# An mLSTM cell and a Fourier-mixed MLP on one core: MLP input products in pairs, the feature transform at half the frequencies, one PSUM pool of four banks

## The chip, the cores and the metric

The kernel runs on one core of a Trainium2 chip. Its engines work side by side, each with a queue of its own that it goes through in order: TensorE (PE in the profile, its weight loads PEld), VectorE (DVE), ScalarE (ACT), GpSimd (POOL) and SyncE (SP), which issues the DMAs here. The metric is the device time of one execution in microseconds, median of the runs. All data is fp32, and each fp32 product shows up in the trace as two weight loads and two matmuls ("passes").

## The reference

An mLSTM cell over 4 batches, 8 heads, 768 steps and 40 features a head gives x of 4 x 768 x 320; then a Fourier mix and an MLP:

```python
for t in range(S):
    m_new = np.maximum(f_gate[:, :, t] + m, i_gate[:, :, t])
    f_stab = np.exp(f_gate[:, :, t] + m - m_new)
    i_stab = np.exp(i_gate[:, :, t] - m_new)
    C = f_stab[:, :, None, None] * C + i_stab[:, :, None, None] * np.einsum('bhd,bhe->bhde', vt, kt)
    n = f_stab[:, :, None] * n + i_stab[:, :, None] * kt
    ...
    y[:, :, t] = o * h_tilde / denom
x = y.transpose(0, 2, 1, 3).reshape(B, S, H * D)
X = np.fft.fft(x, axis=1)
X = np.fft.fft(X, axis=2)
u = x + np.real(X)
mu = np.mean(u, axis=-1, keepdims=True)
var = np.mean((u - mu) ** 2, axis=-1, keepdims=True)
un = (u - mu) / np.sqrt(var + 1e-06)
ch = np.maximum(un @ w_ch1, 0.0) @ w_ch2
out = u + ch
```

w_ch1 is 320 x 1280 and w_ch2 1280 x 320. Both come as 64-bit floats, which the kernel turns into fp32 itself.

## The kernel before, in words

**mLSTM.** Each batch is cut into 6 chunks of 128 steps. A chunk has score products (`ps`, line 405: 40 rows a head, two heads at once in rows 0-39 and 64-103, into two banks), decay weights W (exponentials on ScalarE, a mask on GpSimd, a multiplication with the scores on VectorE, "weighing", line 411), products with the state and with the chunk (`ph`, 419 and 426), an update of the state (`pc`, 435), and a transpose back (`px`, 456) from which VectorE makes x (465 to 471).

**Mix.** x of a whole batch is folded along the sequence and along the features on VectorE (`mix_fold`), then transformed along the sequence (`pz`, `pzt`; the 160 sine and 161 cosine rows over the folded features fill two 128-row blocks and a 64 + 64-row tail). `mix_feat` (line 560) transforms one chunk of 128 tokens along the features: three products of 128 rows by 320 columns into `pu`. The second half of the chunks takes negated copies of the sine tables, which `turn_tables` makes. `mix_add` (569) adds x to `pu`, giving u with its mean and variance; `mix_turn` (579) transposes u (`put`: 128, 128 and 64 features plus the mean as a 65th row), and `mix_turn_out` copies that to the bank of transposed tokens `uT` on ScalarE.

**MLP.** A batch is two groups of three chunks (384 tokens). `mlp_in` (627) computes one of ten blocks of 128 hidden features: three products of 384 columns into `pm` (line 631), the third with 64 feature rows, the mean row and zeros. The mean is taken off there by a row of negated column sums of w_ch1, which `column_sums` (308) computes with four sets of three products (`pw`) and ScalarE copies into `w1_sb`. `mlp_relu` takes even blocks on ScalarE and odd ones on VectorE (in the first group all on ScalarE). `mlp_out` (645) sums ten products of 320 columns for each chunk (`po`, 650), and `mlp_store` scales, adds u and writes out.

**Weights.** A `Piece` of 640 columns is loaded as 64-bit words and turned into fp32 by `split` (281, 283 on VectorE, 284, 285 on ScalarE) and `join` (291, 293, 297 on VectorE). Ten pieces; the last seven fall into batch 0's mix and its first MLP group.

**The order.** It is written out by hand: `at(slot, phase, ...)` puts a piece of work in a slot, and inside a slot the phases are EVAC (copies out of PSUM), FILL (VectorE, ScalarE, GpSimd work), MAIN (MLP products) and FILL_PE (other products). From slot 31 on, each slot holds one `mlp_in` or half an `mlp_out` of batch b, with the mLSTM of batch b + 1 or later and the mix of batch b + 1 laid in between. A transpose `mix_turn` stands one slot behind the addition of its chunk. PSUM has four pools of two banks: scores (`ps_s`), `ph`/`pc`/`px` (`ps_h`), `pz`/`pzt`/`pu`/`put` (`ps_f`), and `pm`/`po` (`ps_m`). A tile waits for the readers of the tile that held its bank.

Of the kernel before, what the change touches and what calls it, by code (L numbers as in the profile page):

```python
# [32 lines left out]
PAD = L + 64  # L33
M_INIT = -1.0e30
# [8 lines left out]
def kernel(  # L43
# [31 lines left out]
    ps_f = pool("ps_f", 2, space=PSUM)  # L75
    ps_m = pool("ps_m", 2, space=PSUM)
# [3 lines left out]
    ones_sb = const.tile([L, 65], FP, name="ones_sb")  # L80
# [5 lines left out]
    dd_sb = const.tile([L, 5, DM], FP, name="dd_sb")  # L86
    fe = const.tile([L, 2, NT // 2, 2 * PAD], FP, name="fe")
    w1_sb = const.tile([L, 3, DFF], FP, name="w1_sb")
# [30 lines left out]
    def gates(gp):  # L119
# [7 lines left out]
        nc.scalar.activation(out=ones_sb[:, 0:1], in_=rest[:, 0:1], func=AF.Exp)  # L127
# [43 lines left out]
        def spread_max(b, c):  # L171

            k = chunks[b, c]
            k.W = wp.tile([L, H, L], FP, name="W", tag="W")
            k.M = []
            for h in range(H):
                if h % NP == 0:
                    k.M.append(ps_f.tile([L, NP, L], FP, name="pM", tag="pf"))
                nc.tensor.matmul(k.M[-1][:, h % NP, :], pick_sb[:, h, :], M[0:H, c, :], start=True, stop=True)  # L179
# [70 lines left out]
        at(4, FILL + 0.5, clear, w1_sb[64:, 2, :], ones_sb)  # L250
        at(4, FILL + 0.6, nc.gpsimd.memset, ones_sb[:, 64:65], -1.0)
        at(7, FILL + 0.5, clear, fe)
        at(10, FILL + 0.5, clear, *(t[64:, 2] for t in uT_bufs))
# [49 lines left out]
    w1_pieces.insert(2, Piece([w1_sb[0:64, 2, 0:part], w1_sb[0:64, 2, part:]], w_ch1[:, 4 * part:]))  # L303
# [4 lines left out]
    def column_sums(f0, n, ps, tag):  # L308

        pw = ps.tile([65, n], FP, name="pw", tag=tag)  # L310
        for ch in range(3):
            r = slice(0, 64 if ch == 2 else L)
            nc.tensor.matmul(pw, ones_sb[r], w1_sb[r, ch, f0:f0 + n], start=(ch == 0), stop=(ch == 2))
        nc.scalar.copy(out=w1_sb[64:65, 2, f0:f0 + n], in_=pw[64:65])

    def load_tables():
        nc.sync.dma_start(out=ds_sb, in_=dft_s)
        nc.sync.dma_start(out=dd_sb[:, 0:3], in_=dft_d)

    def turn_tables():  # L320

        nc.scalar.mul(dd_sb[:, 3], dd_sb[:, 1], -1.0)
        nc.scalar.copy(out=dd_sb[0:64, 4], in_=dd_sb[0:64, 2])
        nc.scalar.mul(dd_sb[64:, 4], dd_sb[64:, 2], -1.0)
# [195 lines left out]
    def mix_seq(b, par):  # L520
# [5 lines left out]
        k.pz = ps_f.tile([L, 2, n], FP, name="pz", tag="pf")  # L526
# [14 lines left out]
    def mix_tail(b, par):  # L541
# [4 lines left out]
        pz = ps_f.tile([L, 1, n], FP, name="pzt", tag="pf")  # L546
# [13 lines left out]
    def mix_feat(b, c):  # L560


        k = mixes[b]
        m = slice(c * L, (c + 1) * L)
        k.pu = ps_f.tile([L, DM], FP, name="pu", tag="pf")
        for n, z in enumerate((k.Z[:, 0, m], k.Z[:, 1, m], k.Zt[:, 0, m])):
            nc.tensor.matmul(k.pu, z, dd_sb[:, n + 2 if c >= NT // 2 and n else n, :], start=(n == 0), stop=(n == 2))  # L567

    def mix_add(b, c):

# [3 lines left out]
        nc.vector.tensor_tensor(out=k.u[:, c, 0:DM], in0=k.pu, in1=xs[b][:, c], op=OP.add)  # L574
        stats = st_p.tile([L, 6], FP, name="stats", tag="stats")
        nc.vector.bn_stats(stats, k.u[:, c, 0:DM])
        nc.vector.bn_aggr(k.u[:, c, DM:DM + 2], stats)

    def mix_turn(b, c):
        k = mixes[b]  # L580
        k.pt = ps_f.tile([L, 3, L], FP, name="put", tag="pf")
        for ch in range(3):
            w = TAIL + 1 if ch == 2 else L
            nc.tensor.transpose(k.pt[0:w, ch, :], k.u[:, c, ch * L:ch * L + w], ident)  # L584

    def mix_turn_out(b, c):
        k = mixes[b]
        uT = uT_bufs[c // TG]
        nc.scalar.copy(out=uT[:, 0:2, c % TG, :], in_=k.pt[:, 0:2, :])  # L589
        nc.scalar.copy(out=uT[0:TAIL + 1, 2, c % TG, :], in_=k.pt[0:TAIL + 1, 2, :])  # L590
# [18 lines left out]
    def plan_mix(b, s0, x_done, s_turn):  # L609
# [17 lines left out]
    def mlp_in(b, gr, f):  # L627
        k = mixes[b]
        k.pm = ps_m.tile([L, TG * L], FP, name="pm", tag="pm")
        for ch in range(3):  # L630
            nc.tensor.matmul(k.pm, w1_sb[:, ch, f * L:(f + 1) * L], uT_bufs[gr][:, ch].rearrange("p c t -> p (c t)"),  # L631
                             start=(ch == 0), stop=(ch == 2))

    def mlp_relu(b, gr, f):
# [4 lines left out]
        if f % 2 and (b, gr) != (0, 0):  # L639
            nc.vector.tensor_scalar(out=ht, in0=k.pm, scalar1=0.0, scalar2=None, op0=OP.max)  # L640
        else:
            nc.scalar.activation(out=ht, in_=k.pm, func=AF.Relu)  # L642
# [57 lines left out]
    at(17, FILL + 0.9, turn_tables)  # L700
    for n, s in enumerate((18, 20, s_mlp + 1, s_mlp + 3)):
        at(s, FILL_PE + 6, column_sums, n * DM, DM, *((ps_m, "pm") if s < s_mlp else (ps_f, "pf")))
# [24 lines left out]
def _dft_d():  # L727

    n = np.arange(HALF_D + 1)
    th = 2.0 * np.pi * ((n[:, None] * np.arange(DM)[None, :]) % DM) / DM  # L730
    c, s = np.cos(th), np.sin(th)

    tail = np.zeros((L, DM))
    tail[0:HALF_D + 1 - L] = c[L:]
    tail[64:64 + HALF_D - 1 - L] = -s[L + 1:HALF_D]
    t = [c[0:L], -s[1:L + 1], tail]
    return np.ascontiguousarray(np.stack(t, axis=1).astype(np.float32))
# [24 lines left out]
def _pack_w1(w):  # L762

    t = w[2 * L:]
# [47 lines left out]
```

## Time and profile before

| | |
|---|---|
| median of 3 runs | 509.38 us (508.55 to 511.45) |
| profiled execution, its own time | 508.07 us |
| its span in the trace | 506.4 us |
| PE busy, instructions | 485.8 us, 2810 |
| DVE busy, instructions | 229.1 us, 550 |
| ACT busy, instructions | 142.5 us, 393 |
| POOL busy, instructions | 93.2 us, 115 |
| DMA | 49.36 MB, 97 GB/s over the span |
| `pm` passes (line 631) | 480, 165.5 us busy, 489 ns each |
| `po` passes (line 650) | 480, 132.4 us busy, 433 ns each |
| `pu` passes (line 567) | 144, 47.5 us busy |

The profile shows one execution. A matmul's duration in the groups (489 ns) contains the way through the array, which overlaps with the next pass; what a pass costs in a row of passes is read from the chain of work that ended last, or from the distance of starts. Line numbers are those of the kernel before; "L631" is line 631. A wait is put down to the instruction whose semaphore came last.

### The profile page before, as it was taken

How to read it: one execution, taken by the hardware profiler on the slowest of the kernel's cores; microseconds unless marked ns; L12 is line 12 of the kernel's file. 1: busy time of each engine (PE TensorE's matmuls, PEld its weight loads, DVE VectorE, ACT ScalarE, POOL GpSimd, SP SyncE). 2: the span in 40 equal slices, each digit the busy share in tenths (PEclk: the TensorE clock that was granted, in tenths of full speed). 3: DMA queues.
4: the chain of work that ended last, by engine and by line, in shares of the span. 5: the costliest groups of instructions: out<-in, count | busy, mean ns of one | idle time of the engine just before them, and what ended most of it. 6: DMA issues, size and time to landing. Idle time of an engine off the chain costs nothing.

```text
span 506.4 us, 7400 instructions
## 1 busy us (share of the span) xinstructions
PE 485.8 (96%) x2810; PEld 345.1 (68%) x2810; DVE 229.1 (45%) x550; ACT 142.5 (28%) x393; POOL 93.2 (18%) x115
## 2 busy tenths in 40 slices
PE   9979788979999999999999999999999999999997
PEld 7767566646777667777677677777667667666564
DVE  6587846898964344248501434348311330311110
ACT  5363435537601435223101334223102110200100
POOL 5375304133300222420000233310000000000000
PEclk9675999999999999999999999999999999999999
DMA  7776970577208641420028541500000000000001
GB/s 228 245 235 218 280 215 0 167 206 206 80 27 241 174 121 70 132 64 0 1 60 254 127 129 64 166 27 1 0 27 13 1 1 26 14 0 26 14 1 38
DMA packets 28579, 49.36 MB, mean 97 GB/s; under 512 B 2872, under 2 KB 19128, under 8 KB 28416
## 3 DMA queue, kind: packets, MB, share of 16 engines
q1 hardware_dynamic: 28544, 48.89, 32.7%
q8 instruction: 22, 0.36, 0.3%
q14 instruction: 13, 0.11, 0.1%
HBM read 44.77 MB, written 4.11 MB: 97 GB/s over the span
## 4 chain that ended last, share of the span: by engine, by line
PE 88%; DVE 9%; DMA 1%; issue 1%; ACT 0%; DVEq 0%; SPq 0%
PE pm L631 30%; PE po L650 26%; PE pu L567 8%; PE ps L405 5%; PE ph L426 4%; PE pz L529 3%; PE ph L419 3%; PE pi L116 2%; PE px L456 2%; PE pzt L550 1%; PE put L584 1%; DVE w_sb L297 1%; PE pM L179 1%; PE pc L435 1%; DMA W<-M_d 1%; DVE W L411 1%
## 5 line engine op out<-in xcount | busy, mean ns | idle before, releaser
L631 PE MATMUL pm<-uT,w_sb 128*128 128x384 f32 x480 | 165.5, 489 | 0.5 <-ACT uT L589 0.5
L650 PE MATMUL po<-w_sb,hT 128*128 128x320 f32 x480 | 132.4, 433 | 0.0
L631 PEld LDWEIGHTS pm<-uT,w_sb 128*128 128x128 f32 x480 | 87.8, 190 | 53.5 <-issue 2.2
L650 PEld LDWEIGHTS po<-w_sb,hT 128*128 128x128 f32 x480 | 90.4, 190 | 37.2 <-issue 0.2
L642 ACT ACTIVATE hT<-pm 128x384 f32<-128x384 f32 x45 | 22.0, 490 | 133.5 <-PE pm L631 133.5
L368 ACT ACTIVATE W<-W,colT 128x128 f32<-128x128 f32 x176 | 54.5, 392 | 0.0
L387 POOL TENSOR_SCALAR_AFFINE_SELECT W<-W 128x1024 f32<-128x1024 f32 x24 | 26.5, 1104 | 148.7 <-ACT W L368 148.6
L656 DVE SCALAR_TENSOR_TENSOR ot<-po,rstd,u 128x320 f32<-128x320 f32 x24 | 13.2, 550 | 86.8 <-PE po L650 86.8
L640 DVE TENSOR_SCALAR hT<-pm 128x384 f32<-128x384 f32 x35 | 19.5, 556 | 54.7 <-PE pm L631 54.6
L441 ACT COPY h<-ph 128x512 f32<-128x512 f32 (+1 forms) x28 | 16.3, 581 | 69.6 <-PE ph L426 69.5
L574 DVE TENSOR_TENSOR u<-pu,x 128x320 f32<-128x320 f32 x24 | 11.8, 491 | 52.3 <-PE pu L567 52.3
L405 PE MATMUL ps<-qk 40*128 40x128 f32 x384 | 33.3, 314 | 1.3 <-DVE W L411 0.7
L405 PEld LDWEIGHTS ps<-qk 40*128 40x128 f32 x384 | 27.9, 214 | 7.2 <-issue 2.1
L411 DVE TENSOR_TENSOR W<-ps,W 128x512 f32<-128x512 f32 x48 | 30.7, 680 | 3.3 <-POOL W L387 3.0
L567 PE MATMUL pu<-dd_sb,Z 128*128 128x320 f32 x96 | 30.7, 442 | 0.7 <-DVE u L574 0.7
L426 PE MATMUL ph<-W,kvt 128*41 128x128 f32 x384 | 28.8, 295 | 2.1 <-DVE W L411 2.1
L589 ACT COPY uT<-put 128x256 f32<-128x256 f32 x24 | 8.9, 372 | 74.9 <-PE put L584 74.9
L381 POOL TENSOR_TENSOR vw<-kvt,colT 128x328 f32<-128x328 f32 x20 | 16.7, 836 | 58.3 <-DMA kvt<-in_kv 34.9
L419 PEld LDWEIGHTS ph<-qg,C 128*128 128x128 f32 x160 | 22.3, 205 | 6.8 <-POOL fe L228 1.8
L419 PE MATMUL ph<-qg,C 128*128 128x128 f32 x160 | 23.2, 292 | 2.5 <-DVE C L449 2.5
L426 PEld LDWEIGHTS ph<-W,kvt 128*41 128x41 f32 x384 | 21.5, 125 | 6.0 <-DVE W L411 2.6
L396 POOL TENSOR_TENSOR C<-C,decB 40x164 f32<-40x164 f32 x32 | 16.7, 522 | 46.6 <-DVE C L449 44.5
(102 smaller groups left out, 458.2 us busy)
## 6 DMA issues: line engine op xcount, KB each, us to landing
W<-M_d SPq DMA_DIRECT2D x22, 512.0 KB
kvt<-in_kv SPq DMA_DIRECT2D x24, 324.0 KB
qk<-in_qkT SPq DMA_DIRECT2D x48, 160.0 KB
raw<-in_w SPq DMA_DIRECT2D x10, 640.0 KB
Gb<-G_d SPq DMA_DIRECT2D x38, 128.0 KB
so<-in_o SPq DMA_DIRECT2D x24, 160.0 KB
out<-ot SPq DMA_DIRECT2D x24, 160.0 KB
ds_sb<-in_dft_s SPq DMA_DIRECT2D x1, 1155.0 KB
```

Of the source, the lines that this page charges most:

```text
L368: nc.scalar.activation(out=k.W[:, h, :], in_=M, func=AF.Exp, scale=-1.0, bias=colT[:, c, 0, b * H + h:b * H + h + 1])
L381: nc.gpsimd.tensor_tensor(out=k.vw, in0=k.v1, in1=colT[:, c, 1, b * H:(b + 1) * H].unsqueeze(2).to_broadcast([L, H, D1]), op=OP.mult)
L387: nc.gpsimd.affine_select(out=k.W, in_=k.W, compare_op=OP.is_ge, fill=0.0, base=0, pattern=[[0, H], [1, L]], channel_multiplier=-1)
L405: nc.tensor.matmul(k.ps[hip][:, p, :], k.qk[r, 1, p, :], k.qk[r, 0, p, :], start=True, stop=True)
L411: nc.vector.tensor_tensor(out=Wv, in0=k.ps[hip], in1=Wv, op=OP.mult)
L419: nc.tensor.matmul(k.ph[:, p, :], k.C[:, p, :], k.qg[:, p, :], start=(p == 0), stop=False, skip_group_check=True)
L426: nc.tensor.matmul(k.ph[hip * 64:hip * 64 + D1, p, :], k.v1[:, 2 * p + hip, :], k.W[:, 2 * p + hip, :], start=(c == 0 and p == 0), stop=Tr ...
L567: nc.tensor.matmul(k.pu, z, dd_sb[:, n + 2 if c >= NT // 2 and n else n, :], start=(n == 0), stop=(n == 2))
L631: nc.tensor.matmul(k.pm, w1_sb[:, ch, f * L:(f + 1) * L], uT_bufs[gr][:, ch].rearrange("p c t -> p (c t)"), start=(ch == 0), stop=(ch == 2))
L640: nc.vector.tensor_scalar(out=ht, in0=k.pm, scalar1=0.0, scalar2=None, op0=OP.max)
L642: nc.scalar.activation(out=ht, in_=k.pm, func=AF.Relu)
L650: nc.tensor.matmul(k.po, k.h[f][:, i * L:(i + 1) * L], w2_sb[:, f, :], start=(f == 0), stop=(f == NFF - 1))
```

## The change

- `mlp_in` works on pairs of blocks. The middle row block of w_ch1 (features 128 to 191, 64 rows) of the even block of a pair lies in partitions 0 to 63 of `w1t_sb`, that of the odd block in 64 to 127. `uT` holds features 0 to 127, then 128 to 191 twice (in both halves), then 192 to 319. A pair is four products of 128 rows and two of 64 rows, the last two next to each other and into different banks.
- The mean is taken off before the transpose: a new `mix_center` writes u minus its mean, with the 64 features doubled, to `uc`. Column sums, their row in `w1_sb` and the clearing of the unused rows go.
- `mix_feat` computes the cosine part at 161 frequencies and the sine part at 159, side by side in one bank: products of 161, 159 and 320 columns. `mix_add` makes the 320 features out of them with four additions, two of which read backwards, and takes the sine part with the other sign in the second half of the chunks. The negated tables go.
- `ps_f` and `ps_m` become one pool of four banks, `ps_m`.
- Both ReLUs of a pair stand in the slot behind the pair's second block; even blocks stay on ScalarE, odd ones on VectorE.

```diff
-    ps_f = pool("ps_f", 2, space=PSUM)
-    ps_m = pool("ps_m", 2, space=PSUM)
+    ps_m = pool("ps_m", 4, space=PSUM)
...
-    w1_pieces.insert(2, Piece([w1_sb[0:64, 2, 0:part], w1_sb[0:64, 2, part:]], w_ch1[:, 4 * part:]))
+    w1_pieces.insert(2, Piece([w1t_sb], w_ch1[:, 4 * part:]))
...
-    def column_sums(f0, n, ps, tag):
-
-        pw = ps.tile([65, n], FP, name="pw", tag=tag)
-        for ch in range(3):
-            r = slice(0, 64 if ch == 2 else L)
-            nc.tensor.matmul(pw, ones_sb[r], w1_sb[r, ch, f0:f0 + n], start=(ch == 0), stop=(ch == 2))
-        nc.scalar.copy(out=w1_sb[64:65, 2, f0:f0 + n], in_=pw[64:65])
-
...
-        k.pu = ps_f.tile([L, DM], FP, name="pu", tag="pf")
-        for n, z in enumerate((k.Z[:, 0, m], k.Z[:, 1, m], k.Zt[:, 0, m])):
-            nc.tensor.matmul(k.pu, z, dd_sb[:, n + 2 if c >= NT // 2 and n else n, :], start=(n == 0), stop=(n == 2))
+        k.pu = ps_m.tile([L, DM], FP, name="pu", tag="pm")
+        nc.tensor.matmul(k.pu[:, 0:NC], k.Z[:, 0, m], dd_sb[:, 0, 0:NC], start=True, stop=False,
+                         skip_group_check=True)
+        nc.tensor.matmul(k.pu[:, NC:], k.Z[:, 1, m], dd_sb[:, 0, NC:], start=False, stop=False,
+                         skip_group_check=True)
+        nc.tensor.matmul(k.pu, k.Zt[:, 0, m], dd_sb[:, 1], start=False, stop=True, skip_group_check=True)
...
-        nc.vector.tensor_tensor(out=k.u[:, c, 0:DM], in0=k.pu, in1=xs[b][:, c], op=OP.add)
+        ops = (OP.subtract, OP.add) if c >= NT // 2 else (OP.add, OP.subtract)
+        u, x, n = k.u[:, c], xs[b][:, c], HALF_D - 1
+        P, Q = k.pu[:, 0:NC], k.pu[:, NC:]
+        nc.vector.tensor_tensor(out=u[:, 0:NC], in0=x[:, 0:NC], in1=P, op=OP.add)
+        nc.vector.tensor_tensor(out=u[:, NC:DM], in0=x[:, NC:], in1=backwards(P, n, n), op=OP.add)
+        nc.vector.tensor_tensor(out=u[:, 1:HALF_D], in0=u[:, 1:HALF_D], in1=Q, op=ops[0])
+        nc.vector.tensor_tensor(out=u[:, NC:DM], in0=u[:, NC:DM], in1=backwards(Q, n - 1, n), op=ops[1])
...
+    def mix_center(b, c):
+
+        k = mixes[b]
+        u = k.u[:, c]
+        k.uc = st_p.tile([L, 2, L + 64], FP, name="uc", tag="uc")
+        twice = bass.AP(tensor=u.tensor, offset=u.offset, ap=[list(u.ap[0]), [L, 2], [1, L + 64]])
+        nc.vector.tensor_scalar(out=k.uc, in0=twice, scalar1=u[:, DM:DM + 1], scalar2=None, op0=OP.subtract)
...
-            w = TAIL + 1 if ch == 2 else L
-            nc.tensor.transpose(k.pt[0:w, ch, :], k.u[:, c, ch * L:ch * L + w], ident)
+            nc.tensor.transpose(k.pt[:, ch, :], k.uc.rearrange("p two n -> p (two n)")[:, ch * L:(ch + 1) * L], ident)
...
-        nc.scalar.copy(out=uT[:, 0:2, c % TG, :], in_=k.pt[:, 0:2, :])
-        nc.scalar.copy(out=uT[0:TAIL + 1, 2, c % TG, :], in_=k.pt[0:TAIL + 1, 2, :])
+        nc.scalar.copy(out=uT_bufs[c // TG][:, :, c % TG, :], in_=k.pt)
...
             t = s_turn(c)
+            at(t, FILL + 0.1, mix_center, b, c)
             at(t, FILL_PE + 5, mix_turn, b, c)
...
-        k.pm = ps_m.tile([L, TG * L], FP, name="pm", tag="pm")
-        for ch in range(3):
-            nc.tensor.matmul(k.pm, w1_sb[:, ch, f * L:(f + 1) * L], uT_bufs[gr][:, ch].rearrange("p c t -> p (c t)"),
-                             start=(ch == 0), stop=(ch == 2))
+        u = [uT_bufs[gr][:, ch].rearrange("p c t -> p (c t)") for ch in range(3)]
+        if f % 2 == 0:
+            k.pm = [ps_m.tile([L, TG * L], FP, name="pm", tag="pm") for _ in range(2)]
+        for i, ch in ((1, 1),) if f % 2 else ((0, 0), (0, 1), (1, 0)):
+            f0 = (f // 2 * 2 + i) * L
+            nc.tensor.matmul(k.pm[i], w1_sb[:, ch, f0:f0 + L], u[2 * ch], start=(ch == 0), stop=False)
+        if f % 2:
+            for i in range(2):
+                r = slice(i * TAIL, (i + 1) * TAIL)
+                nc.tensor.matmul(k.pm[i], w1t_sb[r, f // 2 * L:(f // 2 + 1) * L], u[1][r], start=False, stop=True)
...
-                at(s, EVAC, mlp_relu, b, gr, f)
+                if f % 2:
+                    at(s, EVAC, mlp_relu, b, gr, f - 1)
+                    at(s, EVAC, mlp_relu, b, gr, f)
```

Two places of the order bear on what follows. The first is TensorE's queue in batch 0's first MLP group, from the last feature product of the batch (`pu`, into the sums of chunk 5) on. Before:

```order
L567 MATMUL pu<-dd_sb,Z 128x320 x2
L567 MATMUL pu<-dd_sb,Zt 128x320
L584 MATMUL put<-ident,u 128x128 x2
L584 MATMUL put<-ident,u 65x128
L631 MATMUL pm<-uT_105,w_sb 128x384 x3
L313 MATMUL pw<-w_sb,ones_sb 65x320 x3
L631 MATMUL pm<-uT_105,w_sb 128x384 x3
L456 MATMUL px<-ident,h_114 128x128 x4
L584 MATMUL put<-ident,u 128x128 x2
L584 MATMUL put<-ident,u 65x128
L631 MATMUL pm<-uT_105,w_sb 128x384 x3
```

And of the change, the same stretch:

```order
L550 MATMUL pu<-dd_sb,Z 128x161
L552 MATMUL pu<-dd_sb,Z 128x159
L554 MATMUL pu<-dd_sb,Zt 128x320
L586 MATMUL put<-ident,uc 128x128 x3
L637 MATMUL pm<-uT_103,w_sb 128x384
L641 MATMUL pm<-uT_103,w1t_sb 128x384 x2
L637 MATMUL pm<-uT_103,w_sb 128x384 x3
L440 MATMUL px<-ident,h_112 128x128 x4
L586 MATMUL put<-ident,uc 128x128 x3
L637 MATMUL pm<-uT_103,w_sb 128x384
L641 MATMUL pm<-uT_103,w1t_sb 128x384 x2
```

The two `put` are the transposes of chunks 3 and 4. The column sums are gone, the blocks come as one and three products by turns, and the transposes read `uc`, which VectorE's centering writes, where they read `u`.

The second place is VectorE's queue in the same stretch, behind the addition of chunk 5. Before:

```order
L574 TENSOR_TENSOR u<-pu,x 128x320
L576 BN_STATS stats<-u 128x6
L577 BN_AGGR u<-stats 128x2
L449 TENSOR_TENSOR C_112<-C_112,pc 40x4x41 x2
L291 SCALAR_TENSOR_TENSOR e<-raw,e 128x640
L293 SCALAR_TENSOR_TENSOR m<-raw,m 128x640
L297 TENSOR_TENSOR w_sb<-m,e 128x640
L281 TENSOR_SCALAR e<-raw 128x640
L283 TENSOR_SCALAR m<-raw 128x640
L411 TENSOR_TENSOR W<-ps_1011,W 128x4x128
L411 TENSOR_TENSOR W<-ps_1012,W 128x4x128
L598 TENSOR_SCALAR v<-u 128x6
```

And of the change, from the last of chunk 5's four additions on:

```order
L568 TENSOR_TENSOR u<-u,pu 128x159
L570 BN_STATS stats<-u 128x6
L571 BN_AGGR u<-stats 128x2
L433 TENSOR_TENSOR C_110<-C_110,pc 40x4x41 x2
L289 SCALAR_TENSOR_TENSOR e<-raw,e 128x640
L291 SCALAR_TENSOR_TENSOR m<-raw,m 128x640
L295 TENSOR_TENSOR w_sb<-m,e 128x640
L279 TENSOR_SCALAR e<-raw 128x640
L281 TENSOR_SCALAR m<-raw 128x640
L395 TENSOR_TENSOR W<-ps_1011,W 128x4x128
L395 TENSOR_TENSOR W<-ps_1012,W 128x4x128
L579 TENSOR_SCALAR uc<-u 128x384
```

The centering of chunk 4 (`uc`) stands behind the end of one weight piece, the beginning of the next and a weighing, where the first instruction of the reciprocal root (`v`) stood.

More of the change, by code (lines that the diff above doesn't have):

```diff
@@ L33 @@
 PAD = L + 64
+NC = HALF_D + 1
 M_INIT = -1.0e30
@@ L545, in mix_tail @@
         c0 = 2 * NE if par else 0
-        pz = ps_f.tile([L, 1, n], FP, name="pzt", tag="pf")
+        pz = ps_m.tile([L, 1, n], FP, name="pzt", tag="pm")
         k.pzt = getattr(k, "pzt", []) + [pz]
```

54 lines of the change are left out of this document (21 added, 33 removed).

## The prediction

> **What bounds the kernel now.** I read the page's busy shares, slices and chain first, then the stages, then the chain piece by piece. In the page:
>
> ```profile
> PE 485.8 (96%) x2810; PEld 345.1 (68%) x2810; DVE 229.1 (45%) x550; ACT 142.5 (28%) x393; POOL 93.2 (18%) x115
> ...
> PEclk9675999999999999999999999999999999999999
> ...
> PE 88%; DVE 9%; DMA 1%; issue 1%; ACT 0%; DVEq 0%; SPq 0%
> ```
>
> TensorE (PE) carries the chain, and its granted clock dips only in the first 55 us. The windows by stage (busy time and instruction count of each engine, then clock, DMA share, GB/s) say where PE is the bound and where VectorE (DVE) is:
>
> ```profile
> core 0: us, PE busy (x) PEld busy (x) DVE busy (x) ACT busy (x) POOL busy (x), PEclk, DMA share, GB/s
> ...
> 77.30:99.50 22.20, 20.21 (x160) 14.55 (x160) 16.34 (x37) 10.06 (x29) 7.15 (x8) 1.00 0.28 87
> 99.50:116.40 16.90, 13.23 (x92) 7.84 (x90) 16.06 (x40) 8.10 (x20) 5.40 (x5) 1.00 0.71 195
> 116.40:138.20 21.80, 21.77 (x167) 15.56 (x167) 19.21 (x34) 15.36 (x40) 7.83 (x9) 1.00 0.50 143
> ...
> 155.80:267.20 111.40, 111.40 (x679) 79.59 (x679) 46.36 (x126) 29.64 (x87) 19.94 (x24) 1.00 0.32 93
> ...
> 378.60:490.00 111.40, 111.40 (x416) 73.20 (x415) 23.50 (x60) 11.93 (x31) 0.00 (x0) 1.00 0.03 11
> ```
>
> From about 137 us on, PE never stops: there every product saved is time saved. From 99.5 to 116.4 DVE is busy 16.06 of 16.90 us and PE only 13.23: there a DVE instruction added is time lost, and a product saved is worth nothing.
>
> **The products.** The chain in order of time (start, length, what) gives the price of a pass; an fp32 product is two passes.
>
> ```profile
> 247.18 3.87 PE pm L631 x12
> 251.05 16.15 PE po L650 x60
> ...
> 276.91 2.11 PE pzt L550 x24
> 279.02 2.13 PE pm L631 x6
> 281.15 1.09 PE ps L405 x16
> ```
>
> ```profile
> 167.61 2.13 PE pm L631 x6
> ...
> 172.97 1.61 PE pu L567 x6
> 174.58 1.94 PE pm L631 x6
> ...
> 184.28 0.33 PE put L584 x3
> ...
> 190.43 0.44 PE px L456 x4
> ```
>
> A 384-column pass is 3.87 / 12 = 0.3225 us, a 320-column one 16.15 / 60 = 0.269.
>
> Feature product: 1.61 us now. The new one streams 161 + 159 + 320 columns twice, by the same price per column 2 x (0.136 + 0.134 + 0.269) = 1.08. It saves 0.535 us x 24, of which 18 (batches 1 to 3) lie in the saturated stage: **-9.6 us**.
>
> MLP input: two row blocks cost 12 passes, 3.87 us. The pair does 8 full passes, 2.58 us, and two 64-row products. Whether those run side by side is shown by `ps` (L405), which already pairs rows 0-39 with rows 64-103 in two banks:
>
> ```profile
> 179.98:180.05 0.07, 0.05 (x2) 1.00 0.00 0
> 180.05:180.20 0.15, 0.15 (x2) 1.00 0.00 0
> 180.20:180.28 0.08, 0.08 (x4) 1.00 0.00 0
> ```
>
> In the first 0.05 us of a block two products have started, and the next two start together. The block is 1.09 us for 16 passes of 128 columns; at 0.1075 each that is 8 slots of two, 0.86, and 0.23 for entering. Leaving costs too: a `pm` behind `ps` or `pzt` takes 2.13 instead of 1.94. I take 0.2 for each switch. A pair is then 2.58 + 2 x 0.3225 + 0.4 = 3.625, a saving of 0.245 us. Of the 35 pairs after 137 us two stand right ahead of a `ps` and share its switches (0.645 each): 33 x 0.245 + 2 x 0.645 = **-9.4 us**. The unseen part is that these halves add to a sum already in PSUM, which `ps` doesn't; `pzt` does (24 passes of 193 columns in 2.11 us, two at a time), though from column halves. Bounds for a pair: 3.225 (no switch cost) to 4.27 (no overlap).
>
> The transposes stay at three passes. The column sums (`pw`) go, but lie ahead of 116 us.
>
> **What DVE gets.** Groups by line and shape (busy, mean ns):
>
> ```profile
> L574 DVE TENSOR_TENSOR u<-pu,x 128x320 f32<-128x320 f32 x24 | 11.8, 491 | 52.3 <-PE pu L567 52.3
> L449 DVE TENSOR_TENSOR C<-C,pc 40x164 f32<-40x164 f32 x32 | 10.3, 321 | 20.9 <-PE pc L435 20.4
> L411 DVE TENSOR_TENSOR W<-ps,W 128x512 f32<-128x512 f32 x48 | 30.7, 680 | 3.3 <-POOL W L387 3.0
> ```
>
> One addition of 491 ns becomes four of 160 columns, about 321 ns each by L449: +0.8 us. The centering, 384 columns SBUF to SBUF, isn't in the trace. By L574's price per column, read out of PSUM, 384 columns would take 0.56 us. Undisturbed, L281 does 640 in SBUF in 0.48, and the next instruction starts 0.39 behind it:
>
> ```profile
> 95.53 0.48 DVE L281 TENSOR_SCALAR e<-raw 128x640 uint32<-128x640 uint32 x1
> 95.92 0.48 DVE L283 TENSOR_SCALAR m<-raw 128x640 uint32<-128x640 uint32 x1
> ```
>
> By the columns that leaves some 0.25 as the low end, 0.56 as the high one; L281 is the nearer row (SBUF to SBUF), so I take 0.35. So +1.15 us for each of 24 chunks. In a saturated batch that is 7 us on a DVE busy 46 of 111 us, so it doesn't bind. But the transpose now waits for the centering, which stands in DVE's queue behind the next chunk's four additions. Laying DVE's queue beside PE's in batches 1 and 2, the second, third and sixth transposes come 0.25, 0.6 and 0.9 us too early; batch 3, without mLSTM work, about 0.5. That is **+4 us** (0 to 10).
>
> The four banks: while a pair holds two, the other two serve `pu` and `put`. In order each allocation takes a bank whose reader is a slot old, so I charge nothing; behind it 0.7 us (a ReLU and its handover) per pair if wrong, inside the +10.
>
> **Batch 0's first MLP group.** Here is the cost I think decides. First the gains ahead of it: the first two column sums stood between `ph` and `px`.
>
> ```profile
> 61.45 1.92 PE pw L313 x6
> 63.83 0.59 ACT h L441
> 64.47 0.67 PE px L456 x4
> ```
>
> ScalarE's copy of `h` was queued behind the copy of the sums, so `px` moves 2 us forward; DVE, busy with folding until then, gives back 0.7 of that. Who waited for whom from 77.3 to 99.5 (us, times, longest):
>
> ```profile
> DVE u L574 <- PE pu L567: 7.3, 3, 3.2
> ```
>
> These waits take up part of the 6 x 1.15 = 6.9 us of extras; the saved products shorten them by up to 6 x 0.53 = 3.2. I put the stage's net without clock effects at **-1 us** (-3 to +4). The DVE timeline shows the place from which the trouble comes:
>
> ```profile
> 99.49 0.65 DVE L449 TENSOR_TENSOR C<-C,pc 40x164 f32<-40x164 f32 x2
> ...
> 107.01 0.16 DVE L598 TENSOR_SCALAR v<-u 128x6 f32<-128x6 f32 x1
> ```
>
> Before, the fifth transpose needed only its own addition, long done. Now it needs the centering that is issued at 107.01 in this row order: 2.0 us for the sixth chunk's additions, 7.5 from 99.49 to 107.01, 0.35, some 9.8 us after the sixth `pu`. PE has 0.33 + 1.69 + 1.94 + 0.44 = 4.4 us of work ahead of it. It idles for 5.4 us. The third transpose waits likewise behind a weight split, the fourth chunk's additions and a weighing of 2 x 0.68: about 3.2 us. And without the first two column sums PE has only `px` and four `pz` passes, 1.1 us, from 61.5 to about 67. Idle PE has a price in this trace:
>
> ```profile
> 14.00:17.41 3.41, 3.41 (x27) 3.24 (x28) 3.38 (x6) 1.46 (x2) 0.00 (x0) 1.00 0.47 170
> 17.41:31.06 13.65, 12.01 (x89) 10.24 (x89) 6.71 (x13) 7.36 (x21) 6.41 (x9) 0.50 0.83 264
> 34.48:37.89 3.41, 1.63 (x12) 1.28 (x12) 3.31 (x8) 2.03 (x5) 2.71 (x4) 1.00 0.92 247
> 37.89:51.54 13.65, 12.30 (x107) 10.71 (x108) 9.40 (x19) 5.94 (x20) 6.48 (x9) 0.50 0.68 230
> 99.34:102.75 3.41, 1.76 (x6) 0.66 (x4) 3.28 (x7) 2.25 (x7) 1.93 (x2) 1.00 0.40 63
> ```
>
> After a window of 3.41 us with 1.63 us of work the clock stood at 0.50 for 13.65 us; after one with 1.76 it stayed. (The first drop, at 17.41, followed a busy window, but of products with 8 rows.) The new gaps leave 0.4 to 1.4 us in a window. Each drop takes at most half of 13.65 = 6.8 us from PE. At the third transpose it delays the sixth `pu`, for which DVE stands still: 6.2 us. At the fifth it runs on into the stage that PE bounds: 3.5 us. At 65 us it would cost 5. Two of the three: **+9.7 us** (0 to 15).
>
> The Trainium skill, page "TensorE: Matmul & The Clock Gate", section "Part 1", has the clock halved after an idle window of about 3.4 us and restored after one busy window. This trace differs on both: 1.63 us of work didn't save the clock, and 13.65 us passed with PE busy 12.30. By the page's rule only the 5.4 us gap would count, which is the case of one drop below.
>
> **Sum.** Against the profiled execution, 508.07 us: 508.1 - 9.6 - 9.4 + 4 - 1 + 9.7 = 501.8. That execution lies 1.3 us below the median of the runs, 509.38; I put the forecast at **502.0**.
>
> **Rivals.**
> - No drop: the gaps don't form or fall badly in the windows. 502 - 9.7 = 492.5. For it: after 51.5 us the clock is 1.00 to the end, through windows with 1.76 us of work. Against: the 5.4 us gap follows from the order alone.
> - One drop, 497. The likelier single one is that at the fifth transpose.
> - Three drops, 507, which would be no change.
> - The halves don't overlap, **slower than before**. If the second half can start only behind both passes of the first but one, a pair takes three slots: 35 x 0.3225 = 11.3 more, 513. With no overlap at all (two sums written at once into different banks) 22.6 more, 524. The change turns slower once a pair costs more than 3.625 + 8/35 = 3.85, that is, about what two row blocks cost now. Against it: the two that start together in `ps`, and `pzt`'s rate. The Trainium skill, same page, section "Part 3", says that products start and end strictly in program order; if the two passes of one product stand next to each other in that order, this is the three-slot case. The row of two starts in 0.05 us speaks against it, but doesn't name the halves.
>
> **How the numbers follow.** Two drops 0.40, one 0.20, none 0.13, three 0.12, halves not side by side 0.11, other small outcomes 0.04. A measurement of this kernel can tell about 0.5%, 2.5 us, from no change. Faster by more (under 506.8): 0.75. Same, mostly the three drops: 0.14. Slower (over 511.9): 0.11. The range 492 to 509 leaves out the slower cases and the better part of "none".
>
> **What would show it.** Pairs: a stretch of `pm` in the last group, five pairs, takes 18.1 us instead of 19.4. `pu` with 1.08 us in the chain. A wait of `put` for DVE `uc` of some 5 us near 105 us, and one of 3 near 90; PEclk at half in one or two runs of four windows between 65 and 125. The stage's net stands in the start of the first `po` in the chain:
>
> ```profile
> 136.47 3.70 PE po L650 x13
> ```
>
> It would be some 145 then. If the clock row is whole, the forecast is too high by ten; if a pair takes 4.0 or more, the step on the halves is wrong.

## The result, and the profile after

| | before | changed |
|---|---|---|
| median, timed side by side (4 runs each) | 508.97 us (507.11 to 511.45) | 495.18 us (493.87 to 495.52) |
| profiled execution, its own time | 508.07 us | 495.44 us |
| its span | 506.4 us | 493.4 us |
| start of the first fold on VectorE | 56.57 us | 53.67 us |
| first second-layer product (`po`) in the chain | 136.47 us | 138.49 us |
| from there to the end of the span | 369.9 us | 354.9 us |

The ratio is 0.9721, 95% interval 0.9675 to 0.9768: 2.8% faster. The forecast, 502.0, had the sign but only half of the size, and the time lies inside its range. The last two rows hold the outcome: behind the first `po` the kernel gained 15.0 us, which is just what the prediction summed up for that part (-9.6 - 9.4 + 4); ahead of it, it lost 2.0 us where the prediction had it lose some 8.7.

From the profile's page of the changed kernel, the busy shares, the clock row and the chain by engine:

```profile
PE 460.0 (93%) x2786; PEld 318.9 (65%) x2786; DVE 248.4 (50%) x645; ACT 138.5 (28%) x362; POOL 92.5 (19%) x110
...
PEclk8667988888999999999999999999999999999999
...
PE 78%; DVE 13%; issue 4%; ACT 1%; DMA 1%; POOL 1%; POOLq 0%; DVEq 0%; SPq 0%
```

PE has 25.8 us less to do, DVE 19.3 us more, and DVE's share of the chain has risen from 9% to 13%. The clock row is below 9 in all but one of the first ten slices (to about 123 us); before it was whole from the fifth on. The windows by stage of the changed kernel:

```profile
99.36:117.57 18.21, 12.53 (x85) 7.88 (x84) 16.64 (x42) 7.56 (x18) 5.69 (x5) 0.81 0.65 178
117.57:138.49 20.92, 19.34 (x160) 12.55 (x160) 20.20 (x35) 13.79 (x35) 8.56 (x9) 1.00 0.53 149
157.81:265.18 107.37, 105.95 (x680) 73.00 (x679) 52.03 (x150) 29.35 (x81) 20.40 (x24) 1.00 0.33 96
...
372.54:479.90 107.36, 107.36 (x425) 65.77 (x425) 28.89 (x85) 11.91 (x25) 0.00 (x0) 1.00 0.03 11
```

(Each line: window, its length, then busy time and instructions of PE, PEld, DVE, ACT and POOL, the granted clock, DMA share, GB/s.) A saturated batch takes 107.37 us instead of 111.40. From 99.4 us all the way to the first `po` DVE is now busy for 36.84 of 39.13 us (16.64 + 20.20), PE for 31.87.

The chain of the changed kernel, in order of time:

```profile
138.49 3.70 PE po L659 x13
...
174.10 0.27 PE pu L550 x2
174.38 0.27 PE pu L552 x2
174.65 0.54 PE pu L554 x2
...
455.77 2.58 PE pm L637 x8
458.35 0.85 PE pm L641 x4
459.19 2.78 PE pm L637 x8
461.97 0.84 PE pm L641 x4
...
473.69 16.36 PE po L659 x60
```

A feature product is 0.27 + 0.27 + 0.54 = 1.08 us, as forecast. The five pairs of the last group take 473.69 - 455.77 = 17.92 us, 3.58 each: 3.62 in the middle of the group (forecast 3.625). The four passes of the two 64-row rests take 0.84: two slots of 0.3225 and one switch of 0.2.

What PE waited for: first from 50 to 140 us, then, behind the second mark, from 138 us on (us, times, longest):

```profile
PE put L586 <- DVE v L598: 5.7, 1, 5.7
PE put L586 <- DVE uc L579: 4.6, 2, 2.5
...
PE put L586 <- DVE den L449: 1.9, 2, 0.9
...
PE put L586 <- DVE uc L579: 0.7, 2, 0.3
```

The fifth transposes waited 5.7 us (forecast 5.4; the row names `v`, which stands right behind the centering in DVE's queue: the centering ends at 109.25, the transposes start at 109.40), the second and third 4.6 together, of which the third 2.5 (forecast 3.2, for the third alone), those of batches 1 and 2 2.6 us (forecast 3.5, and 0.5 for batch 3, which waited for nothing). So the gaps are where they were said to be. The windows of the clock around them:

```profile
60.31:63.72 3.41, 0.45 (x3) 0.15 (x2) 3.13 (x11) 0.00 (x0) 0.00 (x0) 1.00 1.04 248
63.72:67.13 3.41, 3.41 (x11) 3.41 (x12) 0.29 (x2) 0.50 (x1) 0.00 (x0) 0.50 1.11 224
73.96:77.37 3.41, 1.88 (x18) 1.26 (x16) 3.31 (x11) 0.87 (x3) 2.80 (x3) 1.00 0.00 0
77.37:80.78 3.41, 3.41 (x37) 3.10 (x36) 0.86 (x3) 0.00 (x0) 0.00 (x0) 0.50 0.00 0
87.61:91.03 3.42, 0.72 (x4) 0.48 (x5) 3.38 (x7) 0.82 (x4) 0.62 (x1) 1.00 0.00 0
91.03:94.44 3.41, 3.41 (x6) 1.88 (x7) 3.20 (x12) 0.95 (x4) 0.00 (x0) 0.50 0.63 188
104.68:108.09 3.41, 0.00 (x0) 0.00 (x0) 3.34 (x4) 1.28 (x2) 2.58 (x2) 1.00 0.80 229
108.09:114.92 6.83, 5.52 (x17) 3.32 (x17) 6.29 (x25) 2.70 (x8) 0.00 (x0) 0.50 0.93 228
```

The clock fell behind all three gaps that the prediction named and behind one more, at 77.4 us. But no stretch lasted 13.65 us: three lasted 3.41 and one 6.83.

### The profile page after: what moved, and what is told of

It is laid out like the page before. It is cut to its first block, busy times and chain, and to the rows that moved or that the text cites. A ratio compares the mean times of both kernels' runs of the same rounds, so it can differ in the third digit from the quotient of the medians.

```text
span 493.4 us, 7413 instructions
## 1 busy us (share of the span) xinstructions
PE 460.0 (93%) x2786; PEld 318.9 (65%) x2786; DVE 248.4 (50%) x645; ACT 138.5 (28%) x362; POOL 92.5 (19%) x110
## 4 chain that ended last, share of the span: by engine, by line
PE 78%; DVE 13%; issue 4%; ACT 1%; DMA 1%; POOL 1%; POOLq 0%; DVEq 0%; SPq 0%
PE po L659 27%; PE pm L637 18%; PE pm L641 6%; PE ps L389 4%; PE ph L410 4%; PE pz L513 4%; PE ph L403 3%; DVE W L395 2%; PE pu L554 2%; PE pi L117 2%; PE pzt L534 2%; PE pu L550 2%; PE put L586 1%; DVE e L289 1%; DMA W<-M_d 1%
## 5 line engine op out<-in xcount | busy, mean ns | idle before, releaser
L637 PE MATMUL pm<-uT,w_sb 128*128 128x384 f32 x320 | 119.7, 503 | 0.9 <-ACT uT L590 0.6
L637 PEld LDWEIGHTS pm<-uT,w_sb 128*128 128x128 f32 x320 | 57.3, 193 | 36.9 <-issue 9.0
L641 PE MATMUL pm<-uT,w1t_sb 64*128 64x384 f32 x160 | 37.4, 544 | 0.0
L590 ACT COPY uT<-put 128x384 f32<-128x384 f32 x24 | 11.5, 479 | 80.8 <-PE put L586 80.8
L389 PE MATMUL ps<-qk 40*128 40x128 f32 x384 | 30.6, 296 | 2.3 <-issue 1.4
L389 PEld LDWEIGHTS ps<-qk 40*128 40x128 f32 x384 | 25.8, 198 | 7.4 <-issue 2.6
L403 PE MATMUL ph<-qg,C 128*128 128x128 f32 x160 | 24.3, 300 | 2.6 <-DVE C L433 2.6
L641 PEld LDWEIGHTS pm<-uT,w1t_sb 64*128 64x128 f32 x160 | 12.2, 187 | 22.3 <-issue 22.3
L380 POOL TENSOR_TENSOR C<-C,decB 40x164 f32<-40x164 f32 x32 | 17.6, 550 | 43.6 <-DVE C L433 41.4
L565 DVE TENSOR_TENSOR u<-x,pu 128x161 f32<-128x161 f32 x24 | 7.7, 321 | 34.9 <-PE pu L554 34.9
```

What stands on the lines that cost most here:

```text
L389: nc.tensor.matmul(k.ps[hip][:, p, :], k.qk[r, 1, p, :], k.qk[r, 0, p, :], start=True, stop=True)
L403: nc.tensor.matmul(k.ph[:, p, :], k.C[:, p, :], k.qg[:, p, :], start=(p == 0), stop=False, skip_group_check=True)
L637: nc.tensor.matmul(k.pm[i], w1_sb[:, ch, f0:f0 + L], u[2 * ch], start=(ch == 0), stop=False)
L641: nc.tensor.matmul(k.pm[i], w1t_sb[r, f // 2 * L:(f // 2 + 1) * L], u[1][r], start=False, stop=True)
```

## The experiments

Each stands with its edit against the changed kernel; times are medians, ratios go against the kernel before, run on the same chip in turn.

**The changed kernel again**, as the yardstick (no edit).

> The changed kernel once more, as the yardstick of the variants beside it. Both theories: 495 +- 1.5 us. The theory that each half-clock stretch ends with the first window of full-row products expects stretches of 3.4 to 6.8 us again behind 55 us, at places that may move by a window; the theory of the prediction, that a stretch lasts 13.65 us whatever follows, expects at least one of 13.65 us there in a second profile.

495.67 us, ratio 0.9771 (0.9731 to 0.9812). Behind 55 us its profile shows half-clock stretches of 10.24 us (at 56.9), 3.41, 3.41 and 6.83; none of 13.65. The first is longer than the 3.4 to 6.8 us expected. The window that lost the clock, and the middle one of the stretch:

```profile
53.46:56.87 3.41, 1.80 (x18) 1.35 (x18) 3.28 (x10) 0.47 (x1) 0.00 (x0) 1.00 1.00 292
60.28:63.70 3.42, 1.17 (x4) 0.66 (x3) 3.14 (x11) 0.00 (x0) 0.00 (x0) 0.50 0.97 210
```

The middle window holds a wait of PE for the fold, with 1.17 us of work; the next one, full, brought the clock back.

**What holds and what restores the clock.** Not the kernel, but products alone, of several kinds, with pauses between them:

```
for rows, cols, both in KINDS:
    pause(16); full(21); burst(48, rows, ...); pause(16); burst(48, rows, ...)
for n, gap in ((2, 1), (1, 1), (1, 2), (1, 3), (2, 6)):
    pause(16); full(21); then: pause(gap); burst(n); pause(gap); burst(n) ...
```

> Not the kernel: products alone, and an output of zeros. For seven kinds of product (128 rows; 64 rows on one row half; 64 rows on both halves in turn; 40 rows on one half and on both; 8 rows; 128 rows with 40 columns of weights) an idle stretch, 21 us of full products, then 31 us or more of the kind without a break, an idle stretch of over 7 us, and the kind again; then full products with pauses of several lengths. It measures how long the granted clock stays at half behind an idle stretch, by kind. Theory of the prediction: 13.65 us for every kind. Theory now: one window of 3.41 us where the products have 128 rows, two or more windows where they have 40 or 8 rows, and with 8 rows the clock falls without any pause, as it did in both profiles at the 8-row products of the start. With pauses: the clock falls where TensorE works under about half of a window, if busy time alone decides.

The windows (PE busy, PEld busy, DVE busy, POOL busy, clock), cut at the clock's own borders:

```profile
78.12:81.53 3.41, 0.00 (x0) 0.00 (x0) 3.20 (x7) 0.00 (x0) 0.50 0.00 0
81.53:84.95 3.42, 2.45 (x4) 1.51 (x5) 0.79 (x2) 0.00 (x0) 0.50 0.00 0
84.95:88.36 3.41, 3.41 (x6) 1.69 (x5) 0.00 (x0) 0.00 (x0) 0.50 0.00 0
88.36:91.77 3.41, 3.41 (x12) 2.06 (x11) 0.00 (x0) 0.00 (x0) 1.00 0.00 0
...
129.32:183.93 54.61, 50.48 (x156) 28.89 (x154) 3.88 (x7) 0.00 (x0) 1.00 0.00 0
183.93:265.85 81.92, 66.72 (x104) 34.65 (x105) 14.04 (x26) 0.00 (x0) 0.50 0.00 0
...
371.66:395.56 23.90, 23.90 (x75) 13.84 (x74) 0.00 (x0) 0.00 (x0) 1.00 0.00 1
395.56:535.50 139.94, 120.61 (x189) 62.10 (x188) 17.92 (x32) 0.00 (x0) 0.50 0.00 0
...
1081.63:1085.04 3.41, 1.73 (x4) 0.52 (x4) 1.43 (x3) 0.00 (x0) 1.00 0.00 0
1085.04:1088.45 3.41, 1.08 (x3) 0.52 (x4) 1.93 (x4) 0.00 (x0) 1.00 0.00 0
1088.45:1091.87 3.42, 2.08 (x4) 0.59 (x3) 1.12 (x2) 0.00 (x0) 0.50 0.00 0
...
1122.59:1126.00 3.41, 3.00 (x5) 1.82 (x6) 0.26 (x1) 0.00 (x0) 0.50 0.00 0
1126.01:1149.90 23.89, 20.24 (x62) 11.34 (x61) 3.29 (x6) 0.00 (x0) 1.00 0.00 1
```

First the 128-row products: they start at 82.50 behind a pause, and the clock is whole again after the first window that they fill (84.95 to 88.36). Then the 64-row ones on one row half: from 129 us on they keep a whole clock whole, but once a pause has halved it at 183.93 they don't bring it back: it stays at half for 81.92 us, of which PE is busy 66.72, until full products come. The 40-row ones lose the clock without any pause (395.56) and stay at half for 139.94 us, pauses included; the 8-row ones do the same at 692.52. Taken on both row halves in turn, 64-row products win the clock back as full ones do, and 40-row ones behave like 64-row ones on one half: they keep it and don't win it back. Products of 128 rows with 40 columns of weights behave like full ones: in this run rows count and columns don't. Last the pauses: a window with 1.73 us of full-row work kept the clock, one with 1.08 lost it; at half, windows with 2.08 and 2.45 us (at 81.53) didn't restore it, one with 3.00 did.

The simplest account of these runs is rows times time. 40 rows all the time are 0.31 of a window and 1.08 us of 128 rows 0.32: both lose. 64 rows all the time are 0.50 and keep it without restoring it. Restoring takes more than 0.72 (2.45 us) and no more than 0.88 (3.00). For losing, the border isn't sharp: in the second profile of the changed kernel the window at 53.46 held 1.80 us of 128-row products (0.53, part of them with 41 columns of weights) and lost the clock all the same. Why isn't known.

This separates the theories. Behind a pause, full-row products had a whole clock again after 10.24 us at half, pause included, so 13.65 us is no fixed length. The stretches of the kernel before had windows in which few-row products took part of the time (32 and 40 rows in those from 17.41 and 20.83, 40 rows in those from 37.89 and 44.72) or PE paused (2.58 and 2.26 us busy in those from 24.24 and 41.31); that this is why they lasted is argued from the run of products alone and wasn't tried in the kernel.

The Trainium skill, page "TensorE: Matmul & The Clock Gate", section "Part 1", has the clock restored after one busy window. This run agrees where the products have 128 rows, and differs for 8 and 40 rows and for 64 rows on one row half. The prediction had set that figure aside on the strength of stretches that such products had partly filled.

**The price of the stretches, first try.**

```diff
+    def keep_busy(out, n):
+        for i in range(n):
+            nc.tensor.matmul(out, ident, ds_sb[:, 0, 0:out.shape[-1]], start=True, stop=True, ...)
 # mix_seq, batch 0, third fold: 4 into a bank of their own; mix_feat, c == 1: 2 into pu
 # mix_turn, batch 0: 2, 3 and 7 into put for c == 1, 2, 4
```

> The changed kernel with full-row products of no use put into five places of batch 0 where TensorE waits (1.3 to 4.5 us of work each, in front of the second product of the third fold, the second feature product and the transposes of the second, third and fifth chunk). Nothing of the result changes. If the half-clock stretches cost what they take from TensorE, the three ahead of the sixth feature product are worth 1.7 us each and the one at 108 us nothing, because VectorE is busy all the way from there to 138 us: the granted clock stays 1.0 behind 55 us and the time falls by 3.5 to 5 us, to about 491. The prediction's pricing (6 us and 3.5 us for the stretches at the third and fifth transposes) would have 485. If the stretches are hidden behind VectorE altogether, the time stays at 495.

494.96 us, ratio 0.9779 (0.9730 to 0.9828): no change that can be told. The profile (of an execution of 491.17 us, the fastest of six) shows why: the seven products ahead of the fifth transposes didn't fill their wait.

```profile
PE put L121 <- ACT hT L662: 5.1, 1, 5.1
```

They themselves waited 5.1 us for the PSUM bank, which ScalarE's ReLU had not yet read, and then ran 7 x 0.645 = 4.5 us ahead of the transposes. The edit added what it took away.

**The price of the stretches, second try**, without those seven.

```diff
-        if b == 0 and c in (1, 2, 4):
+        if b == 0 and c in (1, 2):
```

> The changed kernel with useless full-row products as before, but none ahead of the fifth chunk's transposes, where they waited 5.1 us for a PSUM bank and came too late. If the three half-clock stretches ahead of the sixth feature product are paid at 1.7 us each, they go and the time falls by 3 to 5 us, to 490.5 to 492.5, with the first second-layer product at some 134 us; the stretch at 105 to 115 us stays. If these stretches are hidden behind other waits, or the useless products cost what they save: 495 to 496.

492.18 us, ratio 0.9687 (0.9646 to 0.9729). The windows of its profile up to the sixth chunk's additions, and of its one stretch behind 55 us:

```profile
55.00:95.20 40.20, 34.71 (x273) 26.11 (x273) 29.91 (x83) 14.35 (x36) 8.09 (x9) 1.00 0.55 159
104.45:111.28 6.83, 6.29 (x23) 3.94 (x25) 6.22 (x26) 1.94 (x6) 0.00 (x0) 0.50 0.85 207
```

The clock is whole up to 95 us. From the first fold to the first `po` pass 80.2 us, where the changed kernel took 84.8 and, again, 85.1. So the three stretches ahead of the sixth feature product cost some 4.7 us together, near the expected 1.7 each. This rests on one trace of this version and two of the changed kernel; between the medians lie 3.5 us.

**Centering early.**

```diff
-            at(t, FILL + 0.1, mix_center, b, c)
+            at(s0 + 5 + c, FILL + 0.05, mix_center, b, c)      # and six buffers for uc
```

> The changed kernel with the centering of a chunk issued right behind its additions, not in the slot of its transposes; six buffers for the centred chunk instead of two. If the waits of the transposes are paid where TensorE is the bound, the 2.8 us of idle TensorE in batches 1 and 2 go; in batch 0 the waits of 2.1, 2.5 and 5.7 us shrink to under 1 us, but VectorE has the same work, so that little of the 9 us comes back beyond one or two half-clock stretches of 1.7 us: 495 - 2.8 - 1.7 = 490 to 491. The rival, that the transposes' waits in batch 0 are themselves on the path: 495 - 2.8 - 7 = 485. If the early centering delays the sixth chunk's additions by as much as it frees: 494.

490.17 us, ratio 0.9675 (0.9637 to 0.9713), as its first forecast had it. Its trace takes 81.9 us from the first fold to the first `po` (3 less) and 352.7 from there to the end (2.2 less): the 2.6 us of waits for DVE are gone, and two new ones for a ReLU of ScalarE have come, 1.4 us together. But the fifth transposes still waited 5.7 us, now for something else. What PE waited for, and ScalarE's timeline at the place:

```profile
PE put L587 <- ACT hT L652: 5.7, 1, 5.7
```

```profile
107.59 0.83 ACT L282 ACTIVATE e<-e,ebias 128x640 uint32<-128x640 uint32 x1 [5.32 <-DVE e L279]
108.33 0.72 ACT L283 ACTIVATE m<-m 128x640 f32<-128x640 uint32 x1
108.95 0.85 ACT L652 ACTIVATE hT<-pm 128x384 f32<-128x384 f32 x2
```

The bank for the fifth transposes is one of the first pair's, and the pair's two ReLUs stand in ScalarE's queue behind a weight conversion that waits 5.32 us for DVE's split. In the changed kernel this wait lay under the centering's, equally long: the two ReLUs ended at 109.13, the centering at 109.25.

**The feature transform undone** (three products of 320 columns and one addition as before, on the new pool, with the centering).

```diff
+        for n, z in enumerate((k.Z[:, 0, m], k.Z[:, 1, m], k.Zt[:, 0, m])):
+            nc.tensor.matmul(k.pu, z, dd_sb[:, n + 2 if c >= NT // 2 and n else n, :], ...)
 ...
+        nc.vector.tensor_tensor(out=u[:, 0:DM], in0=k.pu, in1=xs[b][:, c], op=OP.add)
```

> The changed kernel with the old feature transform (three products of 320 columns, one addition), all else as changed. By the sum of the prediction 18 products of 0.535 us come back behind 138 us: +9.6, less up to 1 us of the waits of the transposes, whose additions are shorter; ahead of 138 us six products cost 3.2 us more on TensorE and six additions 3 us less on VectorE, net -2 to +1. 495.5 + 9.6 - 1 = 504 (502.5 to 505). If the feature step's gain were given back in VectorE's four additions: 497.

501.45 us, ratio 0.9859 (0.9807 to 0.9911), 1 us below the expected 502.5 to 505; single runs scattered from 497 to 504. In its trace (of an execution of 503.45 us) the part behind the first `po` takes 363.4 us instead of 354.9: +8.5, of the 8.6 to 9.6 expected there. Ahead of it, 84.0 instead of 84.8.

**The rests of a pair in the same rows.**

```diff
-                r = slice(i * TAIL, (i + 1) * TAIL)
-                nc.tensor.matmul(k.pm[i], w1t_sb[r, f // 2 * L:(f // 2 + 1) * L], u[1][r], ...)
+                nc.tensor.matmul(k.pm[i], w1t_sb[0:TAIL, i, f // 2 * L:(f // 2 + 1) * L], u[1][0:TAIL], ...)
```

> The changed kernel with both 64-row rests of a pair in rows 0 to 63, so that they cannot run side by side; all else as changed. If side by side is what the pairing buys, 35 pairs behind 138 us take 2 slots of 0.3225 us more: +22.6, 518; the five pairs of batch 0's first group are hidden. If the two passes of one half had overlapped the other's only in part (three slots): 11.3 more, 507. If the rows make no difference: 495.5.

The layout of `w1t_sb` follows: both rests lie in partitions 0 to 63, which brings back the second weight join of before (0.83 us on DVE at 39 us, ahead of the first fold). 521.09 us, ratio 1.0285 (1.0244 to 1.0327): slower than before, and 3 us above the expected 518. The chain in the last group:

```profile
481.94 2.78 PE pm L637 x8
484.72 1.48 PE pm L640 x4
```

The four passes now take 1.48 us instead of 0.84, two slots of 0.3225 more: the two rests no longer overlap at all. Behind the first `po` that makes 19.8 us (374.7 against 354.9): 35 x 0.64 = 22.4, less 2.0 us of the transposes' waits, which a slower PE doesn't see, and 0.6 that I can't place. Ahead of it the time rose too, by some 5 us, with longer half-clock stretches there (10.24, 6.83 and 13.65 us); 64-row products that run singly count half in the clock's windows, which fits, and the first group's own five pairs take 5 x 0.64 = 3.2 us more, which its forecast had as hidden; neither was tried apart.

**Three moves more for batch 0**: the rstd chain to the end of the first group, and one weight split a slot later, so that the ReLUs don't stand behind it.

```diff
-        at(s_mlp + 2, FILL + 0.6, mix_rstd, b)
+        at(s_mlp + (NFF - 1 if b == 0 else 2), FILL + 0.6, mix_rstd, b)
-    starts = ... [s_mlp + n for n in (1, 3, 5, 7, 8)]
+    starts = ... [s_mlp + n for n in (2, 3, 5, 7, 8)]      # on top of the early centering
```

> Early centering, and for batch 0 two moves more: the rstd chain (16 small VectorE operations, 2.9 us) from 109 us to the end of the first group, and the weight split of slot 32 one slot later, so that ScalarE's ReLUs of the first pair don't stand behind its conversions. If VectorE bounds 99 to 138 us and the wait for the bank of the fifth transposes comes from the ReLUs: that wait falls from 5.7 us to under 2, the first second-layer product comes 2 to 3 us sooner, 487 to 488. If the early centering took all there was (TensorE bounds the stage behind 117 us): 490.

488.63 us, ratio 0.9629 (0.9588 to 0.9670), between the two forecasts, 487 to 488 and 490. The wait for the bank fell from 5.7 to 2.0 us, but the first `po` then waited 1.1 us for a weight join that the rstd chain had been put in front of. With the chain behind that join (phase FILL + 0.65):

> As the version with early centering, a late rstd chain and the weight split of slot 32 one slot later, but with the rstd chain behind the last weight join, not in front of it, where the second half of the first second-layer product waited 1.1 us for that join. If VectorE's queue sets that place: 1 to 2 us less, 487. If TensorE or the loads set it: no change, 488.5.

488.12 us, ratio 0.9612 (0.9572 to 0.9653). The two versions can't be told apart by time.

**The same with useless products in two waits** (four ahead of the third fold's, two ahead of the second feature product).

> The same, with useless full-row products in two waits of batch 0 (2.6 us of them ahead of the second product of the third fold, 1.1 us ahead of the second feature product). If the half-clock stretch at 63 us costs what it takes from TensorE (3.4 to 6.8 us long), 1.5 to 3 us less than without them: 484 to 485.5. If VectorE hides it: the same as without them.

484.19 us, ratio 0.9532 (0.9490 to 0.9573): the fastest version, 11 us under the changed kernel. Between the traces with and without the products 2.4 us of the gain lie from the first fold to the first `po` (76.0 against 78.4). Between 55 us and its end the clock fell only once, for 3.41 us.

```profile
PEclk9997999998999999999999999999999999999999
```

**The kernel before again.**

> The kernel of before once more, for a second profile. If its clock stays at 1.00 behind 55 us by its order of work and not by luck, no half-clock stretch stands there again, and from the start of the first fold to the first second-layer product pass 79 to 81 us as in the first profile (79.9). If it is the fall of the windows: a stretch of 3.4 to 13.65 us at some place between 55 and 120 us, and up to 5 us more.

507.81 us. Its two half-clock stretches stand where they stood (13.65 us at 16.9 and at 37.4), none behind 55 us, and from the first fold to the first `po` pass 79.4 us (79.9 in the first profile).

The stretches of all traces, from rows like those above (start of the first fold on DVE, start of the first `po`, end of the span):

| | fold at | first `po` at | between | from there to the end |
|---|---|---|---|---|
| before, and again | 56.6, 56.7 | 136.5, 136.1 | 79.9, 79.4 | 369.9, 370.0 |
| changed, and again | 53.7, 53.3 | 138.5, 138.5 | 84.8, 85.1 | 354.9, 354.9 |
| useless products, first try | 50.7 | 134.2 | 83.5 | 354.9 |
| useless products, second try | 54.2 | 134.4 | 80.2 | 354.9 |
| centering early | 55.9 | 137.8 | 81.9 | 352.7 |
| features undone | 54.3 | 138.3 | 84.0 | 363.4 |
| rests in the same rows | 54.2 | 144.0 | 89.8 | 374.7 |
| rstd behind the join | 54.1 | 132.5 | 78.4 | 352.6 |
| the same, useless products | 53.8 | 129.7 | 76.0 | 352.7 |

## Why the prediction was right or wrong

**The products: right.** Pairs at 3.62 us, features at 1.08, both as forecast, and both tried apart: taking the side-by-side away cost two slots a pair, undoing the features 8.5 us behind the first `po`. The rival that the rests don't overlap is out; in the same rows they don't, and that version took 521 us.

That the part behind the first `po` gained 15.0 us to the tenth as summed is partly luck. The waits there came to 2.6 us instead of 4, so the products brought some 17.6 us where the sum had 19.0; where the other 1.4 went isn't shown.

**The waits of the transposes behind 137 us: right, a little large.** 2.6 us instead of 4. With early centering they were gone and this part took 2.2 us less, though 1.4 us of other waits had come.

**What DVE gets: right in kind, a little large.** DVE's timeline of the changed kernel, one chunk's additions, and one centering with the instruction behind it:

```profile
81.70 0.33 DVE L565 TENSOR_TENSOR u<-x,pu 128x161 f32<-128x161 f32 x1 [3.43 <-PE pu L554]
81.94 0.32 DVE L566 TENSOR_TENSOR u<-x,pu 128x159 f32<-128x159 f32 x1
...
82.39 0.32 DVE L568 TENSOR_TENSOR u<-u,pu 128x159 f32<-128x159 f32 x1
82.74 0.49 DVE L570 BATCH_NORM_STATS2 stats<-u 128x6 f32<-128x320 f32 x1
...
95.14 0.41 DVE L579 TENSOR_SCALAR uc<-u 128x384 f32<-128x384 f32 x1
95.46 0.49 DVE L279 TENSOR_SCALAR e<-raw 128x640 uint32<-128x640 uint32 x1
```

Four additions hold the queue for 82.74 - 81.70 = 1.04 us, 0.51 more than the single one of before (84.11 to 84.64), since each starts 0.23 behind the last though it is 0.32 long. I had taken 0.8 from the durations; starts would have given the right price. The centering is 0.32 (95.14 to 95.46) where I took 0.35. Together 0.83 us a chunk, where 1.15 was charged.

**Four banks at nothing: wrong in one place, without effect on the sum.** With early centering the fifth transposes waited 5.7 us for a bank, as long as for the centering before. The working looked at whose reader is a slot old and not at what stands ahead of that reader in ScalarE's queue.

**Batch 0's first MLP group: the step that failed.** "Each drop takes at most half of 13.65 = 6.8 us from PE", and from it +9.7 us for two of three places. The gaps came, the clock fell at all three places and once more, but each stretch ended with the first window that PE filled. What failed is the length: 13.65 us was read off two stretches in which products of few rows and pauses had filled part of the windows, and was taken as fixed. Measured, the stretches lasted 3.41 and 6.83 us, and the three ahead of the sixth feature product cost 4.7 us together, not the 5 and 6.2 us that the prediction put on two of them. The one at 108 us I had charged with 3.5; the profile has DVE busy for 36.84 us from 99.4 to 138.5, with PE waiting for it again at the end, so it should cost nothing, which is argued from the trace and wasn't tried by itself: the useless products put there delayed the transposes instead.

**The stage without the clock: right within 1.5 us.** From the first fold to the first `po` the second try with useless products took 80.2 us, 0.3 more than before; -1 was forecast, within -3 to +4.

**What was not in the sum.** The first fold starts 2.9 us sooner than before. In ten traces of versions that share the changed kernel's beginning, or nearly all of it, it starts at 50.7 to 55.9 us, mostly near 54; in both of before at 56.6 and 56.7. The prediction priced nothing ahead of 61 us. The second weight join that went (0.82 us) can't be the cause alone: the version with the rests in the same rows still has it and starts its fold at 54.2. This part stays open.

Together: 9.7 - 4.7 = 5.0 too much for the stretches, 2.9 not seen, 1.3 the other way in the stage. 501.8 - 5.0 - 2.9 + 1.3 = 495.2; the profiled execution took 495.44. So the size was off by two parts of one sign, of which the stretches are explained and the earlier fold is not. Two small slips in the working changed nothing: on the scale of the median the sum is 503.1, not 502.0, and a pair could have cost 7.4/35 us more before the change turned slower, not 8/35.

## What to carry to other kernels

Where a cost is read off an earlier event of the trace, ask what filled it: the stretches of before held products of 32 and 40 rows and pauses, the new ones mostly full-row products, and the shapes in the trace could have told the two cases apart. One trace can divide a change's effect by stage: where a change saves products in a saturated part and adds work in a part with another bound, compare the two parts from a shared event, not the end. And when a wait is taken away, look for a second one of the same length underneath; here a bank stood under the centering.

## What the runs showed of the hardware

- The clock changes at borders 3.41 us apart, or whole multiples of that, in all these traces. In the run of products alone rows times time told what happened: it was lost at 0.32 of a window and below, kept at 0.50, not restored at 0.72 and restored at 0.88. In the kernel a window of 0.53 lost it once (1.80 us at 53.46), so the border of the loss is open. 64-row products on one row half keep a whole clock and yet don't win it back.
- Useless full-row products in a wait paid: 3.5 us of 495.7 in one version (11 products), 3.9 of 488.1 in another (6), by the medians. With seven more that themselves waited for a bank the gain was gone (494.96).
- The same program up to the first fold reached it at times up to 5 us apart. The clock's stretches ahead of it fall differently from run to run, which may be why; it wasn't tried. The size is about that of the spread of one version's times (492.8 to 496.7 for the changed kernel).
